# Reordering exp and the key products of a decode block's softmax part, and spreading its weight gradients over more heads

## The chip, the cores and the metric

The kernel runs on one core of one Trainium2 chip. The metric is the device time of one launch in microseconds (us), lower is better. A core has TensorE (PE, matrix products; PEld in a profile is its loading of weights), VectorE (DVE), ScalarE (ACT), GpSimd (POOL) and SyncE (SP), each with its own instruction queue that runs in order. They work in the on-chip memory SBUF; matrix products land in PSUM. Transfers between the device's memory and SBUF are issued here by SP (loads and four small stores) and by POOL (large stores); 16 DMA engines carry them.

## The reference

The block is one decode step of attention and an MLP with residuals, and what is timed is the forward pass together with the gradients of everything but one unused input. There are 2 batch entries, one query each, 32 heads, a cache of 4096 keys and values of 128 elements per head, a model width of 640 and an MLP width of 1728, all in bf16.

```python
x = A_x                                    # [2, 1, 640]
q = layernorm(x) @ wq                      # 32 heads x 128
p = softmax(q . k_cache * 128**-0.5)       # per pair (batch, head): 4096 probabilities
o = p @ v_cache
h = x + o @ wo
out = h + relu(layernorm(h) @ w1) @ w2
out, vjp = jax.vjp(f, x, k_cache, v_cache, wq, wo, w1, w2)
return out, *vjp(grad_out)
```

The gradients of the two caches are by far the largest outputs: one [4096, 128] array per pair for the keys and one for the values. For a pair they are outer products, gV = p x go and gK = gs x q * scale with gs = p * (V go - dot). The gradients of wq, wo, w1 and w2 are outer products of two vectors per batch entry, summed over the batch.

## The kernel before

Work goes by the 64 pairs of batch and head. A pair's K or V (1 MB) lies in one SBUF buffer of [128 partitions, 32 rows, 128]. Ten such buffers (`NBIG`) are shared by two classes: "ld" for loads, "g" for gradients on their way out. `take` and `give` hand them out in order; `pump` issues the next load of a fixed list as soon as a load buffer is given back in program order, and SP waits until the last reader is done.

**The first pass**, `p1_iter(i)` (L437 to 557), is a software pipeline over pairs with three in work at once: `c` is pair i (scores), `p` is pair i-1 (exponentials and products), `r` is pair i-2 (sums over values). It is a generator of eight stages, k = 0 to 7. Between two stages the caller may insert second-pass and background work, so the order of instructions on each engine is the order in which the program issues them; nothing is rescheduled (`manual_schedule`).

- K is transposed on PE in four groups of eight blocks (`transpose_group`, L373 to 383, PSUM tile `t_ps`, two buffers). Each group is copied to SBUF (`t_sb`) by ACT (L382), apart from the fourth of the first 33 iterations, which DVE copies (L380). `matvec_group` (L388) then multiplies by q, giving the scores `s`.
- Stage 1: PE sums over the rows of the scaled keys of `r` (`u_rows`, L465, one set of four products for each half of `pk`), spreads the maximum of `p` over partitions (L483), and DVE takes the minimum of it, giving the bias `nb` (L485).
- Stage 3: ACT computes `ep = exp(SCALE * s + nb)` with the sum `esum` (L502). It stands after the copy of the third key group (stage 2). At the end of stage 3 ACT copies `ep` into the column 128 of two tiles `pk` (L513).
- Stage 4: `pk_half(0)` (L452), a DVE product of half of the keys with `ep`. Stage 5: reciprocal of the total and the normalised probabilities (L533, L534). Stage 6: the maximum of `c`'s scores (L542), then `pk_half(1)`, after which the key buffer is given back.
- `m_part(0..7)` (L445) accumulates value rows against `pk` for `r`, four rows in each part, spread over all stages; stage 7 gives the value buffer back and ACT copies the result out (L553, L554).

**The second pass**, `p2_iter(j)` (L777 to 830), reads V again as a tile `Wt`. It transposes it on PE as fp32 (L398), with ACT copies (L403), multiplies it by `go` (L411), and DVE writes gK and gV by halves (L772). POOL stores them (L810, L829).

**The plan** (L1014 to 1026): iterations i = 0 to 43 run the first pass alone; from i = 44 to 65 every other iteration also carries one head of the second pass ("mixed"); the 53 other heads run by themselves ("the last part"). The first 32 pairs are batch entry 0. After i = 33 and i = 65 a background generator `middle_gen` computes attention output, layer norm, MLP, and the vector `go` of each head, which the second pass needs. Its long reductions on DVE are `ttr` (L622).

**Background work** runs by credit. `bg_step(k, rate)` adds `rate` to a queue's credit, at most 2, and lets the queue's generator run until the credit is used; each `yield` of a generator says what it used (0.5 where it says nothing). Three queues exist: `bg` (middle parts), `bg2` with the rate `RATE2` (weight gradients, `fin_gen`, L936 to 972), and `bg3` with 0.6 (`gx_gen`, the gradient of x through wq, L882 to 934). `fin_gen` starts in the last part, once the MLP of batch entry 1 is done, and goes through a fixed list:

- vectors are laid out as rows by `rows_of` (1.7 credits for four column groups: two yields of 0.5 and one of 0.7)
- `outer_rows` makes the outer products of the four weights: PE products of 2 rows (L872), ACT copies out of PSUM (L877), and a store by POOL (L879). Two products cost 1.0. The outputs come in the order out_7 (w2), out_6 (w1), out_5 (wo), out_4 (wq)
- before the rows of wo's gradient it waits for the vector `gh1` of batch entry 1, and before those of wq's for the last group of `go`
- last come the layer norm's gradient and two row stores of out_1

In the last part each head calls all three queues seven times. `gx_gen` reloads wq in six tiles `wqs` (L891) and holds each for `at[k]`, 18 steps after issue, before it transposes it (L916).

Of the kernel before, what the change touches and what calls it, by code (L numbers as in the profile page):

```python
# [7 lines left out]
FP32 = mybir.dt.float32  # L8
BF16 = mybir.dt.bfloat16
ALU = mybir.AluOpType  # L10
ACT = mybir.ActivationFunctionType
# [4 lines left out]
def kernel(  # L16
# [20 lines left out]
    nc = tc.nc  # L37
# [7 lines left out]
    NSC = Sk // 128  # L45
# [3 lines left out]
    SCALE = 0.08837890625  # L49
# [3 lines left out]
    HALF = NSC // 2  # L53
# [12 lines left out]
    small = ctx.enter_context(tc.tile_pool(name="small", bufs=3))  # L66
# [5 lines left out]
    def pst(shape, dtype, tag, name):  # L72
        return ps.tile(shape, dtype, tag=tag, bufs=PSB[tag], name=name)
# [11 lines left out]
    def balance():  # L85
        for a, b, wrong in (("ld", "g", lambda: count["ld"] > target[0]), ("g", "ld", lambda: count["ld"] < target[0])):
            while wrong() and free[a] > 0:
                homes[b].insert(0, homes[a].pop())
                for d in (free, count):
                    d[a] -= 1  # L90
                    d[b] += 1

    def take(tag, shape, name):
        assert free[tag] > 0, (tag, name)
        free[tag] -= 1
        k = homes[tag].pop(0)
        t = pools.get(k, big).tile(shape, BF16, tag=f"big{k}", bufs=1, name=name)
        home_of[id(t)] = (tag, k, t)
        return t

    def give(t):
        tag, k, _ = home_of.pop(id(t))
        free[tag] += 1
        homes[tag].append(k)
        balance()

    step = [0]
# [193 lines left out]
    pkp = tc.alloc_tile_pool(name="pkp", bufs=1)  # L301
# [83 lines left out]
    def matvec_group(dst, t_sb, g, vec):  # L385
        for j in range(GT):
            sc = g * GT + j
            nc.tensor.matmul(dst[:, sc:sc + 1], lhsT=t_sb[:, j, :], rhs=vec, start=True, stop=True)  # L388
# [48 lines left out]
    def p1_iter(i, dve_group, busy):  # L437

        c = S1[i] if i < NP1 else None
        p = S1[i - 1] if 1 <= i <= NP1 else None  # L440
        r = S1[i - 2] if i >= 2 else None

        def m_part(k):
            for sc in range(4 * k, 4 * k + 4):
                nc.tensor.matmul(r["m"][:, 0:129], lhsT=r["V"][:, sc, :],  # L445
                                 rhs=r["pk"][sc // HALF][:, sc % HALF, 0:129],
                                 start=(sc == 0), stop=(sc == NSC - 1))

        def pk_half(k):

            sl = slice(k * HALF, (k + 1) * HALF)
            nc.vector.tensor_tensor(  # L452
                out=p["pk"][k][:, :, 0:128].rearrange("p s (a two) -> p s a two", two=2),
                in0=p["K"][:, sl, :].rearrange("p s (a two) -> p s a two", two=2),
                in1=p["ep"][:, sl, None, :].to_broadcast([128, HALF, 64, 2]), op=ALU.mult)

        def u_rows(h):


            if h == 0:  # L460
                u_bank[0] = pst([128, 512], FP32, "u", "u_ps")
            for t in range(2):
                for g in range(4):
                    sc = 16 * t + 4 * g
                    nc.tensor.matmul(u_bank[0][32 * g:32 * g + 32, :], lhsT=onehot[:, 31 - h:63 - h],  # L465
                                     rhs=r["pk"][t][:, 4 * g:4 * g + 4, 0:128],
                                     start=(h == 0 and t == 0), stop=(h == H - 1 and t == 1))

        if c is not None:
            b, h = pairs[i]  # L470
            q = qc[:, h, b:b + 1]
            c["KT0"] = transpose_group(c["K"], 0, busy=busy)
            c["KT1"] = transpose_group(c["K"], 1)
        yield
        if r is not None:
            r["m"] = pst([128, 132], FP32, "m", "m_ps")
            u_rows(pairs[i - 2][1])
        if p is not None:

            bp, hp = pairs[i - 1]  # L480
            bhp = bp * H + hp
            mx = p["bank"][:, 64:192]
            nc.tensor.matmul(mx, lhsT=p["rmax"][:].to_broadcast([128, 128]), rhs=nident[:], start=True, stop=True)  # L483
            nb = small.tile([128, 1], FP32, tag="nb", name="nb")
            nc.vector.tensor_reduce(out=nb[:], in_=mx, op=ALU.min, axis=AX.X)  # L485
        if r is not None:
            m_part(0)
        yield
        if c is not None:
            c["bank"] = pst([128, 512], FP32, "sps", "s_ps")  # L490
            c["s"] = c["bank"][:, 0:NSC]
            matvec_group(c["s"], c.pop("KT0"), 0, q)
            c["KT2"] = transpose_group(c["K"], 2, busy=busy)
        if r is not None:
            m_part(1)
        yield
        if c is not None:
            matvec_group(c["s"], c.pop("KT1"), 1, q)
        if p is not None:
            ep = small.tile([128, NSC, 2], BF16, tag="ep", name="ep")  # L500
            esum = small.tile([128, 1], FP32, tag="esum", name="esum")
            nc.scalar.activation(out=ep[:], in_=p["s"][:, :, None].to_broadcast([128, NSC, 2]),  # L502
                                 func=ACT.Exp, bias=nb[:], scale=SCALE, accum_out=esum[:])
            p["ep"] = ep
        if r is not None:
            m_part(2)
        if c is not None:
            c["KT3"] = transpose_group(c["K"], 3, dve_group)
        if p is not None:
            p["pk"] = []  # L510
            for k in range(2):
                pk = pkp.tile([128, HALF, 130], BF16, tag="pK", bufs=3, name="pk")
                nc.scalar.copy(out=pk[:, :, 128:129], in_=ep[:, k * HALF:(k + 1) * HALF, 0:1])  # L513
                p["pk"].append(pk)
        yield
        if p is not None:
            pk_half(0)
        if r is not None:
            m_part(3)
        if c is not None:  # L520
            matvec_group(c["s"], c.pop("KT2"), 2, q)
        if r is not None:
            m_part(4)
        if p is not None:

            totp = p["bank"][:, 256:257]
            nc.tensor.matmul(totp, lhsT=half_f32, rhs=esum[:], start=True, stop=True)
        yield
        if r is not None:
            m_part(5)  # L530
        if p is not None:
            rtot = rt[:, bp, hp:hp + 1]
            nc.vector.reciprocal(out=rtot, in_=totp)  # L533
            nc.vector.tensor_scalar(out=P_bf[:, bhp, :], in0=ep[:, :, 0], scalar1=rtot,  # L534
                                    scalar2=None, op0=ALU.mult)
        yield
        if r is not None:
            m_part(6)
        if c is not None:
            matvec_group(c["s"], c.pop("KT3"), 3, q)  # L540
            rmax = small.tile([128, 1], BF16, tag="rmax", name="rmax")
            nc.vector.reduce_max(out=rmax[:], in_=c["s"], axis=AX.X)  # L542
            c["rmax"] = rmax
        if p is not None:
            pk_half(1)
            give(p["K"])
        yield
        if r is not None:
            br, hr = pairs[i - 2]
            m_part(7)  # L550
            give(r["V"])
            MT = mats.tile([128, 128], BF16, tag="MT", bufs=NMT, name="MT")
            nc.scalar.activation(out=MT[:], in_=r["m"][:, 0:128], func=ACT.Copy, scale=rt[:, br, hr:hr + 1])  # L553
            nc.scalar.activation(out=OU[:, br, hr, 0:1], in_=r["m"][:, 128:129], func=ACT.Copy, scale=rt[:, br, hr:hr + 1])  # L554
            MTs[(br, hr)] = MT
            del S1[i - 2]
        yield
# [324 lines left out]
    def gx_gen(fin, gx1):  # L882
# [3 lines left out]
        def load(k):  # L886
            hn = min(QP, H - k * QP)
            while free["ld"] < 1:
                yield 0.0
            tiles[k] = take("ld", [128, ND, QP * 128], "wqs")  # L890
            nc.sync.dma_start(out=tiles[k][:, :, 0:hn * 128],  # L891
                              in_=wq_r[:, :, k * QP * 128:(k * QP + hn) * 128])
            at[k] = step[0] + 18

        at = {}
        for k in range(NQ):
# [117 lines left out]
    M0_ITERS = 10  # L1014
    P2_AT = H + 2 + M0_ITERS
    RATES = (0.2, 0.6, 0.2, 0.8, 0.45)
    RATE2 = 1.0
    plan = []
    i = j = 0
    while i <= NP1 + 1 or j <= NP1:  # L1020
# [55 lines left out]
    for n, (i, j) in enumerate(plan):  # L1076
# [26 lines left out]
        if i is None:  # L1103
            spread[0] = 2
            k = 0
            while g2 is not None:
# [4 lines left out]
                bg_step(0, rate)  # L1111
                bg_step(1, RATE2)
                bg_step(2, 0.6)
            continue
        at = MIXED if j is not None else REST
        for k, _ in enumerate(p1_iter(i, i < H + 1, 2 if H + 1 < i < H + 5 else 0)):
# [14 lines left out]
            bg_step(0, rate)  # L1131
            bg_step(1, RATE2)
        if i is not None and i in (H + 1, NP1 + 1):
# [41 lines left out]
```

## Time and profile before

| What | Value |
|---|---|
| Time, median of 8 runs | 955.39 us (951.59 to 962.02) |
| Time of the profiled execution | 953.29 us |
| Its span, first to last instruction | 951.5 us |
| PE busy | 771.5 us, 81% |
| DVE busy | 654.8 us, 69% |
| ACT busy | 574.0 us, 60% |
| POOL busy | 114.1 us, 12% |
| Bytes moved | 372.37 MB, mean 391 GB/s |
| Mean granted PE clock | 0.784 |

In the page's slices each digit is the busy share of one fortieth of the span in tenths; `PEclk` is the PE clock that was granted, in tenths of full speed, and the line GB/s what the DMA engines moved. Stages in time: the first pass for batch entry 0 until about 218 us; the first pass alone beside the middle of batch entry 0 until about 310 us; the mixed part until about 490 us; the last part after that. Stores of the weight gradients (L879) run from 569.4 to 821.6 us; the two row stores of out_1 are issued at 862.5 and 877.3 us; the last gK is issued at 937.4 us.

In a list of waits each row is: engine, tile and line that waited, what released it, then total us, number of times, longest us. In the order of time each row is: start us, duration us, engine, line, operation, output and input, and in brackets the idle time of the engine before it and its releaser. In a table by stretch each engine has busy us and a count.

### The profile page before, as it was taken

Reading aid. Unit: us, or ns where it says so; the run is one execution under the profiler, and the core shown is the slowest. Engines: PE = TensorE matmul, PEld = TensorE weight load, DVE = VectorE, ACT = ScalarE, POOL = GpSimd, SP = SyncE. Lnnn points to the kernel's source line nnn. Section 1 sums busy time; section 2 is a strip of 40 time slices with the busy share of each in tenths; the row PEclk is TensorE's granted clock in tenths of the full one; section 3 lists DMA queues with packets and bytes.
Section 4 is the critical chain, followed back from the end, with each engine's and each line's share of the span. In section 5 each row is a group of like instructions: output and inputs, shape, how many; then the busy total and the mean of one; then the engine's idle time right before and its main releaser. Section 6 shows DMA issues by size and latency. Waiting matters only on the chain.

```text
span 951.5 us, 27206 instructions
## 1 busy us (share of the span) xinstructions
PE 771.5 (81%) x11643; PEld 650.9 (68%) x11643; DVE 654.8 (69%) x1235; ACT 574.0 (60%) x1250; POOL 114.1 (12%) x220
## 2 busy tenths in 40 slices
PE   5999999989888989889787888778885679856670
PEld 4888878878777878778776866565574565545560
DVE  4566877855496977868659886586499744556683
ACT  3666666657577767767534466677763568733340
POOL 1000000000000110100102211121132211121131
PEclk8999999999799999999887555575575765665565
DMA  8999999999685999999999999999999999999996
GB/s 348 409 401 404 410 404 411 408 418 386 226 306 226 361 425 422 421 403 424 399 410 399 395 423 370 362 393 421 389 404 423 421 423 421 414 424 421 417 424 287
DMA packets 62952, 372.37 MB, mean 391 GB/s; under 512 B 5776, under 2 KB 19280, under 8 KB 21232
## 3 DMA queue, kind: packets, MB, share of 16 engines
q1 hardware_dynamic: 42176, 221.50, 58.5%
q0 software_dynamic: 20656, 149.14, 37.8%
q8 instruction: 91, 1.49, 0.6%
q14 instruction: 29, 0.24, 0.1%
HBM read 221.48 MB, written 149.13 MB: 389 GB/s over the span
## 4 chain that ended last, share of the span: by engine, by line
PE 38%; DMA 25%; DVE 21%; ACT 7%; issue 7%; POOL 1%; POOLq 0%; ACTq 0%; DVEq 0%
DVE pk L452 10%; PE t_ps L398 10%; DMA out_dram<-gV 9%; DMA Vt<-in_A_v_cache_dram 6%; PE m_ps L445 6%; PE t_ps L377 6%; DMA Kt<-in_A_k_cache_dram 4%; DVE gV L772 3%; DMA wqs<-in_A_wq_dram 3%; PE o_ps L872 3%; DMA out_dram<-ot 3%; PE dp_ps L411 2%; PE s_ps L388 2%; PE u_ps L465 2%; ACT t_sb L403 2%
## 5 line engine op out<-in xcount | busy, mean ns | idle before, releaser
L382 ACT COPY t_sb<-t_ps 128x1024 bf16<-128x1024 bf16 x223 | 219.5, 1015 | 62.8 <-PE t_ps L377 61.0
L398 PE MATMUL t_ps<-ident_f,Wt 128*128 128x128 f32 x1024 | 223.9, 366 | 0.3 <-ACT t_sb L918 0.3
L445 PE MATMUL m_ps<-pk,Vt 128*128 128x129 bf16 x2048 | 197.9, 223 | 14.5 <-DMA Vt<-in_A_v_cache_dram 14.4
L403 ACT COPY t_sb<-t_ps 128x512 f32<-128x512 f32 x256 | 148.2, 588 | 91.9 <-PE t_ps L398 88.3
L398 PEld LDWEIGHTS t_ps<-ident_f,Wt 128*128 128x128 f32 x1024 | 162.6, 190 | 18.3 <-issue 8.5
L452 DVE TENSOR_TENSOR pk<-Kt,ep 128x2048 bf16<-128x2048 bf16 x128 | 156.1, 1220 | 21.0 <-ACT ep L502 20.9
L772 DVE TENSOR_TENSOR gK<-rb,gsp 128x2048 bf16<-128x2048 bf16 x128 | 152.3, 1228 | 21.1 <-DMA out_dram<-gK 19.1
L772 DVE TENSOR_TENSOR gV<-rb,pp 128x2048 bf16<-128x2048 bf16 x128 | 152.4, 1220 | 15.7 <-DMA out_dram<-gV 8.8
L377 PE MATMUL t_ps<-ident_bf,Kt 128*128 128x128 bf16 x2048 | 152.9, 225 | 3.1 <-DMA Kt<-in_A_k_cache_dram 2.9
L445 PEld LDWEIGHTS <-Vt 128*128 128x128 bf16 x2048 | 134.5, 101 | 15.9 <-DMA Vt<-in_A_v_cache_dram 15.3
L411 PEld LDWEIGHTS <-t_sb 128*128 128x128 bf16 x2048 | 93.3, 106 | 73.9 <-ACT t_sb L403 62.0
L411 PE MATMUL dp_ps<-gom,t_sb 128*128 128x2 bf16 x2048 | 95.1, 167 | 47.1 <-ACT t_sb L403 46.4
L377 PEld LDWEIGHTS <-Kt 128*128 128x128 bf16 x2048 | 126.9, 101 | 5.1 <-DMA Kt<-in_A_k_cache_dram 3.3
L829 POOL DMA_DIRECT2D out_dram<-gV x64 | 34.2, 534 | 514.1 <-DVE gV L772 427.7
L388 PE MATMUL s_ps<-qc,t_sb 128*128 128x1 bf16 x2048 | 87.9, 164 | 1.3 <-ACT t_sb L382 0.9
L388 PEld LDWEIGHTS <-t_sb 128*128 128x128 bf16 x2048 | 79.3, 97 | 3.3 <-ACT t_sb L382 2.0
L877 ACT CAST ot<-o_ps 128x512 bf16<-128x512 f32 (+4 forms) x160 | 68.5, 480 | 20.1 <-PE o_ps L872 17.6
L785 DVE SCALAR_TENSOR_TENSOR gsp<-dp_ps,negdot,P_bf 128x64 bf16<-128x64 f32 x64 | 18.0, 281 | 86.3 <-PE dp_ps L411 85.9
L799 ACT CAST rb<-dp_ps 128x256 bf16<-128x256 f32 x64 | 24.0, 375 | 79.4 <-DVE gK L772 51.7
L465 PE MATMUL u_ps<-pk,onehot 128*32 128x512 bf16 x512 | 48.5, 396 | 20.8 <-DVE pk L452 20.1
L810 POOL DMA_DIRECT2D out_dram<-gK x64 | 34.0, 532 | 238.7 <-DVE gK L772 198.0
L380 DVE COPY t_sb<-t_ps 128x1024 bf16<-128x1024 bf16 x33 | 22.8, 692 | 51.8 <-PE t_ps L377 51.8
(204 smaller groups left out, 795.7 us busy)
## 6 DMA issues: line engine op xcount, KB each, us to landing
Kt<-in_A_k_cache_dram SPq DMA_DIRECT2D x64, 1024.0 KB, 13.0
Vt<-in_A_v_cache_dram SPq DMA_DIRECT2D x64, 1024.0 KB, 13.3
Wt<-in_A_v_cache_dram SPq DMA_DIRECT2D x64, 1024.0 KB, 12.7
out_dram<-gV POOLq DMA_DIRECT2D x64, 1024.0 KB, 13.6
out_dram<-gK POOLq DMA_DIRECT2D x64, 1024.0 KB, 13.1
wo_t<-in_A_wo_dram SPq DMA_DIRECT2D x4, 1280.0 KB, 19.8
out_dram<-ot POOLq DMA_DIRECT2D x5, 1024.0 KB, 11.8
wq_t<-in_A_wq_dram SPq DMA_DIRECT2D x5, 960.0 KB, 13.9
```

What stands on the lines that cost most here:

```text
L377: nc.tensor.transpose(t_ps[:, j, :], nat[:, g * GT + j, :], ident_bf[:])
L382: nc.scalar.copy(out=t_sb[:], in_=t_ps[:])
L388: nc.tensor.matmul(dst[:, sc:sc + 1], lhsT=t_sb[:, j, :], rhs=vec, start=True, stop=True)
L398: nc.tensor.transpose(t_ps[:, j, :], natf[:, 2 * cc:2 * cc + 2, :].rearrange("p c k -> p (c k)"), ident_f[:])
L403: nc.scalar.copy(out=t_sb[:], in_=t_ps[:])
L411: nc.tensor.matmul(dst[:, sc:sc + 2], lhsT=v[:, j, :, par], rhs=vecs[:, par, :], start=(par == 0), stop=(par == 1))
L445: nc.tensor.matmul(r["m"][:, 0:129], lhsT=r["V"][:, sc, :], rhs=r["pk"][sc // HALF][:, sc % HALF, 0:129], start=(sc == 0), stop=(sc == NSC ...
L452: nc.vector.tensor_tensor(out=p["pk"][k][:, :, 0:128].rearrange("p s (a two) -> p s a two", two=2), in0=p["K"][:, sl, :].rearrange("p s (a ...
L465: nc.tensor.matmul(u_bank[0][32 * g:32 * g + 32, :], lhsT=onehot[:, 31 - h:63 - h], rhs=r["pk"][t][:, 4 * g:4 * g + 4, 0:128], start=(h == ...
L772: nc.vector.tensor_tensor(out=pairs_view(dst[:, sl, :]), in0=row.rearrange("p (a two) -> p a two", two=2)[:, None, :, :].to_broadcast([128 ...
L829: nc.gpsimd.dma_start(out=natural(out_3, b, h), in_=gV[:])
L877: nc.scalar.copy(out=ot[0:P, k, n0:n0 + nn], in_=o_ps[0:P, 0:nn])
```

## The change

Four things are moved or altered:

1. exp of `p` goes from stage 3 to the head of stage 2, ahead of the third key group's copy.
2. `pk_half(0)` goes from the head of stage 4 to the end of stage 3, in front of the yield; `pk_half(1)`, with the give-back of the key buffer, from the end of stage 6 to stage 5, in front of the reciprocal. The tile `pk` and its ACT copy are made inside `pk_half`, one at a time.
3. `RATE2` goes from 1.0 to 0.55.
4. The wait for a reloaded wq tile goes from 18 to 22 steps.

```diff
         def pk_half(k):
 
+            pk = pkp.tile([128, HALF, 130], BF16, tag="pK", bufs=3, name="pk")
+            nc.scalar.copy(out=pk[:, :, 128:129], in_=p["ep"][:, k * HALF:(k + 1) * HALF, 0:1])
+            p["pk"].append(pk)
             sl = slice(k * HALF, (k + 1) * HALF)
...
             c["s"] = c["bank"][:, 0:NSC]
-            matvec_group(c["s"], c.pop("KT0"), 0, q)
-            c["KT2"] = transpose_group(c["K"], 2, busy=busy)
-        if r is not None:
-            m_part(1)
-        yield
-        if c is not None:
-            matvec_group(c["s"], c.pop("KT1"), 1, q)
         if p is not None:
             ep = small.tile([128, NSC, 2], BF16, tag="ep", name="ep")
             esum = small.tile([128, 1], FP32, tag="esum", name="esum")
             nc.scalar.activation(out=ep[:], in_=p["s"][:, :, None].to_broadcast([128, NSC, 2]),
                                  func=ACT.Exp, bias=nb[:], scale=SCALE, accum_out=esum[:])
             p["ep"] = ep
+        if c is not None:
+            matvec_group(c["s"], c.pop("KT0"), 0, q)
+            c["KT2"] = transpose_group(c["K"], 2, busy=busy)
+        if r is not None:
+            m_part(1)
+        yield
+        if c is not None:
+            matvec_group(c["s"], c.pop("KT1"), 1, q)
         if r is not None:
             m_part(2)
         if c is not None:
             c["KT3"] = transpose_group(c["K"], 3, dve_group)
         if p is not None:
             p["pk"] = []
-            for k in range(2):
-                pk = pkp.tile([128, HALF, 130], BF16, tag="pK", bufs=3, name="pk")
-                nc.scalar.copy(out=pk[:, :, 128:129], in_=ep[:, k * HALF:(k + 1) * HALF, 0:1])
-                p["pk"].append(pk)
-        yield
-        if p is not None:
             pk_half(0)
+        yield
         if r is not None:
             m_part(3)
...
             m_part(5)
         if p is not None:
+            pk_half(1)
+            give(p["K"])
+        if p is not None:
             rtot = rt[:, bp, hp:hp + 1]
...
             c["rmax"] = rmax
-        if p is not None:
-            pk_half(1)
-            give(p["K"])
         yield
...
-            at[k] = step[0] + 18
+            at[k] = step[0] + 22
...
-    RATE2 = 1.0
+    RATE2 = 0.55
```

More of the change, by code (lines that the diff above doesn't have):

```diff
@@ L491, in p1_iter @@
             c["s"] = c["bank"][:, 0:NSC]
+        if p is not None:
+            ep = small.tile([128, NSC, 2], BF16, tag="ep", name="ep")
+            esum = small.tile([128, 1], FP32, tag="esum", name="esum")
+            nc.scalar.activation(out=ep[:], in_=p["s"][:, :, None].to_broadcast([128, NSC, 2]),
+                                 func=ACT.Exp, bias=nb[:], scale=SCALE, accum_out=esum[:])
+            p["ep"] = ep
+        if c is not None:
             matvec_group(c["s"], c.pop("KT0"), 0, q)
@@ L498, in p1_iter @@
             matvec_group(c["s"], c.pop("KT1"), 1, q)
-        if p is not None:
[L500 to L504, printed above, removed]
         if r is not None:
@@ L510, in p1_iter @@
             p["pk"] = []
-            for k in range(2):
-                pk = pkp.tile([128, HALF, 130], BF16, tag="pK", bufs=3, name="pk")
-                nc.scalar.copy(out=pk[:, :, 128:129], in_=ep[:, k * HALF:(k + 1) * HALF, 0:1])
-                p["pk"].append(pk)
+            pk_half(0)
         yield
-        if p is not None:
-            pk_half(0)
         if r is not None:
@@ L531, in p1_iter @@
         if p is not None:
+            pk_half(1)
+            give(p["K"])
+        if p is not None:
             rtot = rt[:, bp, hp:hp + 1]
@@ L543, in p1_iter @@
             c["rmax"] = rmax
-        if p is not None:
-            pk_half(1)
-            give(p["K"])
         yield
```

## The prediction

> **What bounds the kernel now.** I read the page's second part first, since its slices separate the stages.
>
> ```profile
> PE   5999999989888989889787888778885679856670
> DVE  4566877855496977868659886586499744556683
> PEclk8999999999799999999887555575575765665565
> GB/s 348 409 401 404 410 404 411 408 418 386 226 306 226 361 425 422 421 403 424 399 410 399 395 423 370 362 393 421 389 404 423 421 423 421 414 424 421 417 424 287
> ```
>
> A slice is 23.8 us. From 0 to about 230 us the DMA moves some 405 GB/s (softmax part, first 32 heads). Slices 11 to 14 (238 to 333 us) fall to 226 to 361: compute alone sets the pace. From 333 us it is mostly 421 to 425, with a second dip at 560 to 700 us. Where the DMA is full, shortening compute buys nothing; the gain must come from the dips, and from 541 us on the total is bytes over rate.
>
> Second, the busy time by stretch (columns: PE, PEld, DVE, ACT, POOL busy with counts, granted clock, DMA share, GB/s):
>
> ```profile
> 192.00:218.00 26.00, 24.71 (x466) 21.81 (x467) 14.43 (x33) 16.09 (x35) 0.00 (x0) 0.93 1.01 416
> 273.36:279.80 6.44, 6.05 (x119) 5.38 (x117) 5.91 (x18) 5.12 (x11) 0.00 (x0) 1.00 0.85 327
> 580.00:600.00 20.00, 15.74 (x132) 12.69 (x133) 12.39 (x26) 12.58 (x33) 3.55 (x8) 0.50 0.99 362
> 600.00:620.00 20.00, 15.77 (x117) 9.67 (x116) 10.27 (x14) 14.75 (x32) 3.42 (x7) 0.50 0.96 359
> 680.00:700.00 20.00, 16.96 (x158) 13.06 (x157) 13.69 (x23) 12.31 (x32) 3.95 (x8) 0.50 0.94 364
> 700.00:760.00 60.00, 40.33 (x560) 34.67 (x558) 54.89 (x84) 31.18 (x64) 15.71 (x27) 0.73 1.02 421
> ```
>
> To be seen: one softmax iteration of the first dip (6.44 us) has PE at 94% and DVE at 92%, so only a few tenths of a microsecond per iteration are loose. The DMA share cannot tell the second dip from a full queue (0.99 at 362 GB/s, 1.02 at 421), so I go by GB/s.
>
> Third, the waits of 254 to 294 us, and the order of one iteration there on ACT and DVE:
>
> ```profile
> DVE pk L452 <- ACT ep L502: 7.5, 6, 3.4
> PE u_ps L465 <- DVE pk L452: 3.2, 5, 0.9
> ...
> 270.18 1.01 ACT L382 COPY t_sb<-t_ps 128x1024 bf16<-128x1024 bf16 x1 [1.15 <-PE t_ps L377]
> 271.08 0.32 ACT L502 ACTIVATE ep<-s_ps,nb 128x64 bf16<-128x64 f32 x1
> 271.53 1.23 DVE L452 TENSOR_TENSOR pk<-Kt,ep 128x2048 bf16<-128x2048 bf16 x1 [0.47 <-ACT ep L502]
> 272.67 0.75 DVE L622 CUSTOM_DVE_ANT_0 junk<-w_t,fbc 128x576 bf16<-128x576 bf16 x1
> 273.35 0.17 DVE L533 RECIPROCAL rt<-s_ps 128x1 f32<-128x1 f32 x1
> 273.87 1.22 DVE L452 TENSOR_TENSOR pk<-Kt,ep 128x2048 bf16<-128x2048 bf16 x1
> ```
>
> The loop: third key group's copy, exp, first key product, one background reduction, three small operations, second key product, the u_rows matmuls of PE (they wait 0.39 to 0.85 us for it), the maximum, the next third group.
>
> **The change, part by part.**
>
> *Exp ahead of the third copy.* Nothing is added. The bias nb is ready at 269.59 (269.30 + 0.29); the third group's PSUM at 270.14. Exp (0.32, plus 0.20 for the accumulator read) fits ACT's 1.15 us idle time, about 269.66 to 270.18, and the copy starts about when it did. Cover gone: where nb is late the copy waits behind exp. In the first 32 heads, once background reductions run, nb ends some 0.3 us later than the copy's PSUM and the third group's matvec moves by about 0.25 us. In the mixed part (310 to 490 us) ACT is busy with the first two copies until 345.5 while nb ends at 345.35, so exp costs the copy its own 0.5 us; behind it stand the fourth copy and PE's matvec of the third group. The mixed part runs at 421 to 425 GB/s, which hides this; if it did not, 0.3 us in 11 iterations is 3 us.
>
> *First key product at once.* DVE had been free since 271.06, so of its 0.47 us wait nearly all goes. In the first 32 heads the fourth copy is on DVE (0.69 us) directly ahead of it and still is: gain nothing.
>
> *Second key product ahead of reciprocal, P and maximum.* It starts up to 0.45 us earlier there (0.16 + 0.24 + 0.19, overlapped: 71.47 against 71.02 in one iteration). The maximum now comes after it and PE's broadcast of it waits. First part, the loop from the fourth copy's start: 0.61 to the first product, 1.13 to the second, 1.14 to the reciprocal, 0.19 + 0.16 to the maximum, 0.25 to PE's broadcast, 2.27 to the next copy: 5.75 against 6.06 us, so 0.31, not 0.45. In the dip DVE's own list (1.14 + 0.68 + 0.2 + 0.15 + 0.07 + 0.10 + 1.13 + 0.74 + 0.21 + 0.79 + 0.76) is 5.97 us against 6.44: at most 0.47.
>
> *Queues.* SP's reload of a key buffer waits for this product; it moves earlier with it, and value or W loads queued behind it on SP too. No DMA is added, POOL's order is untouched. The two ones-columns copies of ACT (some 0.2 us each) split; the second needs m_part(3), which has run by then.
>
> *What reaches the end.* Up to 192 us nothing: PE waits 2.0 us there for a key load, so the DMA dates that point. From 198 to 218 us 3.5 iterations x 0.31 = 1.1 us (ceiling: PE's idle 1.3). From 254 to 293 us PE idles 0.80 + 0.38 + 0.85 + 0.39 + 0.78 + 0.76 = 3.96 us; the loop sets that idle time, but DVE stops it at 0.47 an iteration, so I take 5 x 0.46 = 2.3 us. Part one: **3.4 us, between 0 and 5.3**; zero if the layer-norm chain (236 to 254 us, PE idle 2.9) and the first W group's forced chain (293 to 302) swallow it.
>
> *Weight gradients spread.* RATE2 is the credit a background step gives. The generator's costs add to 134: 97 (out_7, out_6, out_5), then 37 (GQ rows, out_4). A head has 7 steps. Before: 97/7 = 14 heads, an idle stretch till the last GQ group (head 41), then 37/7 = 5.3 heads; the trace shows those stores from 569 to 693 us and from 792 to 822 us. After: 97/0.55/7 = 25 heads, 37/0.55/7 = 9.6: heads 17 to 53 without a gap. Nothing is added.
>
> At 560 to 700 us a head carries 6.6 units (9.95 us: 541 to 693 for 15.3 heads), and the DMA loses against 421: 26 x 20 + 59 x 20 + 62 x 20 + 17 x 20 + 57 x 20 (395, 362, 359, 404, 364 GB/s) = 4.4 MB, **10.5 us**. After, 3.85 units a head. With no units a head takes at most 6.8 us (nine heads, 693 to 754), so linearly 6.8 + 3.15 x 3.85/6.65 = 8.6 us. The DMA needs, for 36 heads of 3.15 MB, 14.9 MB of gradients and 5.2 MB of wq, 133 MB / 421 = 317 us: 8.8 a head. Compute is just under the DMA, too close to recover all: I take 0.63 of 10.5, **6.6 us**, with 10.5 above and a loss below.
>
> *Wait of 22 steps for wq.* Its PE stalls (7.4 us at 730.7, 6.5 at 755.1) shrink, but the DMA ran at 421 then: 0. It and the slower rate push the last row store from head 54 to about 60.5 of 64: 3.5 heads left. If they were gone, out_4's rest would be a tail of 10 us or more.
>
> **Two rules weighed.** Row first: 700 to 760 us moved 421 GB/s. [...] by the row 6.6 more. The row decides. Second: the clock was 0.50 at 580 to 620 us with PE 79% busy, and 0.73 at 700 to 760 with 67%. [...] the filled heads 32 to 41 run their transposes at half clock (1.09 instead of 0.64 us per four, 1.8 us a head, 18 us over ten heads). I allow half clock: the 9.95 us heads had it already.
>
> **Sum.** 3.4 + 6.6 = 10.0 us against the profiled execution's 953.3 (span 951.5 and 1.8 around it): 943.3. The median is 2.1 us above that execution, so **945.4**.
>
> **Rivals.** (1) *Spreading is hidden, only the loop gains*: 955.4 - 3.4 = 952.0. For it: the DMA share of 0.96 to 1.02 in the dip. Against: its GB/s. (2) *The loop change is hidden, spreading works*: 948.8. For it: the chain runs over PE at 218 to 236 us (PE 97% busy), and the third part takes what is left. (3) *Slower*: the filled last part becomes compute-bound. Heads 17 to 53 took 329 us, 9.1 a head; the chain matmul, ACT eviction, next matmul (PE waits 15.0 us for evictions at 560 to 700) then stands in all 36 heads, beside the W transposes at half clock. At 9.5 us a head it costs 36 x 0.4 = 14 less 3.4: 966. It decides from 9.2 us a head. For it: PE 79 to 85% busy at 0.50. Against: the linear 8.6.
>
> **How the numbers follow.** Forecast 0.55, rival 1 0.14, rival 2 0.11, rival 3 0.20. About 0.5% (4.8 us) is what this kernel's measurement can tell from no change. The forecast holds 940 to 949, almost all faster; rival 2 is faster in half of its cases; rival 1 mostly within. Faster 0.60, same 0.20, slower 0.20. The forecast's low end with all 10.5 and 5.3 is 939.6, less 2 us of spread; the high end takes rival 1 and the mild side of rival 3: 938 to 958.
>
> **What would show it.** Right: the idle time of DVE's first product on ep gone at 254 to 293 us and iterations of some 6.0 us; exp ahead of the third copy with that copy's wait unchanged; first dip 3 us shorter; gradient stores evenly from about 575 to 860 us, with 410 GB/s or more at 560 to 700; last row store well before the last gK. Wrong: ACT's third copy late behind nb, heads 32 to 53 above 9 us at less than 421 GB/s, or a slower first part.

## The result and the profile after

The changed kernel takes **945.66 us** (median of 11 runs, 941.68 to 950.13) beside 955.81 for the kernel before (32 runs); the ratio is 0.9894, 95% interval 0.987 to 0.9918. The forecast was 945.4. The total is right, but the profile shows another split of it: that the sum came out is luck. Its execution takes 945.39 us (span 943.6; before 953.29 and 951.5).

The page's slices (23.6 us each), after:

```profile
PE   5999999989899989799798866857687786766670
DVE  4666777856688968678759787766957557445683
PEclk8999999999999989999975575656755568557565
GB/s 348 409 397 407 410 405 410 407 419 410 288 308 268 407 424 421 424 391 422 421 421 334 421 422 384 383 374 412 406 424 420 422 406 421 425 409 399 423 422 262
```

The eleventh slice (236 to 260 us) has risen from 226 to 288 GB/s and its clock from 7 to 9, the fourteenth from 361 to 407. The second dip is still there (slices 25 to 27, 566 to 637 us). Busy time by stretch, after (columns as in the prediction):

```profile
192.00:218.00 26.00, 25.38 (x478) 22.21 (x479) 14.50 (x29) 17.31 (x37) 0.00 (x0) 0.94 1.02 420
254.00:293.00 39.00, 36.43 (x726) 32.64 (x724) 33.43 (x94) 30.73 (x66) 0.00 (x0) 1.00 0.72 272
...
560.00:580.00 20.00, 15.22 (x118) 11.60 (x117) 17.45 (x28) 11.19 (x27) 3.83 (x9) 0.50 1.02 414
580.00:600.00 20.00, 15.20 (x121) 11.89 (x122) 11.71 (x21) 11.73 (x29) 3.13 (x7) 0.50 1.00 370
600.00:620.00 20.00, 14.93 (x182) 12.62 (x181) 15.61 (x25) 11.50 (x31) 3.12 (x7) 0.67 1.00 372
620.00:640.00 20.00, 12.94 (x94) 8.77 (x93) 11.54 (x20) 10.98 (x23) 3.13 (x7) 0.50 0.99 386
640.00:700.00 60.00, 44.76 (x537) 36.20 (x536) 47.05 (x72) 38.39 (x92) 11.63 (x23) 0.67 1.01 413
```

The order in the loop is the intended one. ACT and DVE in one iteration of the first dip, after (start and length in us):

```profile
262.71 0.29 DVE L488 TENSOR_REDUCE nb<-s_ps 128x1 f32<-128x128 f32 x1
...
262.91 0.76 DVE L621 CUSTOM_DVE_ANT_0 junk<-w_t,fbc 128x576 bf16<-128x576 bf16 x1
...
263.03 0.31 ACT L498 ACTIVATE ep<-s_ps,nb 128x64 bf16<-128x64 f32 x1
...
263.36 1.01 ACT L382 COPY t_sb<-t_ps 128x1024 bf16<-128x1024 bf16 x1
...
264.39 1.22 DVE L455 TENSOR_TENSOR pk<-Kt,ep 128x2048 bf16<-128x2048 bf16 x1
...
266.20 1.22 DVE L455 TENSOR_TENSOR pk<-Kt,ep 128x2048 bf16<-128x2048 bf16 x1
...
267.34 0.17 DVE L535 RECIPROCAL rt<-s_ps 128x1 f32<-128x1 f32 x1
```

The exponentials run 0.33 us ahead of the third copy, and neither product waits: DVE fills the time with background reductions (the L621 lines). Where the 7.9 us of the span came from is read off the start of the maximum in each softmax iteration, and of the store of gV in each head of the second pass (trace, us; heads 0 to 10 lie in the mixed part):

| Point | Before | After | Gained so far |
|---|---|---|---|
| iteration 32 | 218.09 | 218.39 | -0.3 |
| iteration 33 | 223.78 | 222.65 | 1.1 |
| iteration 35 | 241.33 | 240.17 | 1.2 |
| **iteration 36** | 252.03 | 246.65 | **5.4** |
| iteration 42 | 293.57 | 286.22 | 7.4 |
| head 0 | 313.73 | 305.20 | 8.5 |
| head 17 | 539.07 | 531.86 | 7.2 |
| head 53 | 868.74 | 860.44 | 8.3 |
| head 63 | 934.79 | 926.87 | 7.9 |

In this pair of traces the whole gain is there by head 0. Behind that point one trace is a weak witness: the trace of the spreading alone, told below, runs the program of the kernel before up to the last part, keeps step with it up to iteration 42 (0.2 us), and is 5.8 us behind at head 10. Heads 17 to 53, over which the weight gradients now spread, take 328.6 us instead of 329.7, but not evenly: the changed kernel is 28.0 us ahead at head 32 and 7.8 at head 44. And more than half of the gain comes from a single iteration, to which the forecast gave nothing. Its stretch, first before, then after:

```profile
236.00:240.00 4.00, 3.36 (x60) 3.04 (x59) 3.13 (x21) 3.05 (x10) 0.00 (x0) 1.00 0.95 387
240.00:244.00 4.00, 1.70 (x37) 1.17 (x37) 2.90 (x6) 0.88 (x1) 0.00 (x0) 0.96 0.43 107
244.00:248.00 4.00, 4.00 (x54) 3.45 (x52) 0.82 (x1) 1.32 (x3) 0.00 (x0) 0.50 0.88 356
248.00:252.00 4.00, 4.00 (x78) 3.97 (x76) 1.40 (x7) 1.28 (x3) 0.00 (x0) 0.50 0.35 145
```

```profile
236.00:240.00 4.00, 2.57 (x46) 1.93 (x43) 3.53 (x18) 2.72 (x7) 0.00 (x0) 1.00 0.65 262
240.00:244.00 4.00, 3.94 (x94) 3.41 (x94) 1.85 (x4) 1.47 (x4) 0.00 (x0) 1.00 0.86 311
244.00:248.00 4.00, 3.68 (x88) 3.47 (x85) 2.23 (x8) 1.87 (x6) 0.00 (x0) 1.00 1.00 356
248.00:252.00 4.00, 3.12 (x61) 2.46 (x59) 0.68 (x2) 3.53 (x7) 0.00 (x0) 1.00 0.98 391
```

Before, PE is "4.00 busy" at 244 to 252 us at a granted clock of 0.50, and iteration 36 takes 10.70 us. After, the clock stays at 1.00 and it takes 6.48. What precedes it is PE's wait for the key products. PE's timeline, before and then after (the bracket is the idle time and what ended it):

```profile
241.12 0.40 PE L465 MATMUL u_ps<-pk,onehot 128*32 128x512 bf16 x4 [1.76 <-DVE pk L452]
242.70 0.40 PE L465 MATMUL u_ps<-pk,onehot 128*32 128x512 bf16 x4 [1.18 <-DVE pk L452]
```

```profile
239.96 0.40 PE L468 MATMUL u_ps<-pk,onehot 128*32 128x512 bf16 x4 [1.43 <-DVE pk L455]
```

Before, both products stand behind some twenty small layer-norm operations on DVE, and PE waits 1.76 and 1.18 us for them. After, the first product runs ahead of that chain and one wait of 1.43 us is left.

Two theories are left. **Mine after the traces**: the loop's edits give all of the gain, some 8 us, about half of it by keeping PE's clock up once (1.00 instead of 0.50 at 244 to 252 us); the spreading gives nothing, because the second dip is made by slow transfers and not by compute. **The forecast's**: 3.4 us from the loop and 6.6 from the spreading.

### The profile page after: what moved, and what is told of

Read it like the earlier page. It is cut to its first block, busy times and chain, and to the rows that moved or that the text cites. A ratio compares the mean times of both kernels' runs of the same rounds, so it can differ in the third digit from the quotient of the medians.

```text
span 943.6 us, 27268 instructions
## 1 busy us (share of the span) xinstructions
PE 765.8 (81%) x11643; PEld 647.6 (69%) x11643; DVE 655.6 (69%) x1235; ACT 573.0 (61%) x1250; POOL 112.3 (12%) x220
## 4 chain that ended last, share of the span: by engine, by line
DMA 34%; PE 31%; DVE 16%; issue 12%; ACT 4%; POOL 1%; POOLq 0%; DVEq 0%; ACTq 0%
DMA out_dram<-gV 13%; DMA Vt<-in_A_v_cache_dram 10%; PE m_ps L445 8%; PE t_ps L377 8%; DMA out_dram<-gK 7%; DVE pk L455 5%; DVE gV L771 5%; DMA out_dram<-ot 4%; PE t_ps L398 3%; PE s_ps L388 3%; DVE gK L771 2%; PE u_ps L468 2%; ACT t_sb L382 2%; PE t_ps L369 1%; DVE junk L621 1%
## 5 line engine op out<-in xcount | busy, mean ns | idle before, releaser
L398 PE MATMUL t_ps<-ident_f,Wt 128*128 128x128 f32 x1024 | 227.3, 368 | 1.4 <-ACT t_sb L917 0.7
L455 DVE TENSOR_TENSOR pk<-Kt,ep 128x2048 bf16<-128x2048 bf16 x128 | 153.0, 1223 | 18.7 <-PE m_ps L445 12.7
L552 ACT ACTIVATE MT<-m_ps,rt 128x128 bf16<-128x128 f32 x64 | 23.5, 368 | 60.3 <-PE m_ps L445 60.3
L621 DVE CUSTOM_DVE_ANT_0 junk<-wo_t,hbc 128x640 bf16<-128x640 bf16 x64 | 52.4, 818 | 0.2
```

The lines of the kernel that those rows point to most:

```text
L398: nc.tensor.transpose(t_ps[:, j, :], natf[:, 2 * cc:2 * cc + 2, :].rearrange("p c k -> p (c k)"), ident_f[:])
L455: nc.vector.tensor_tensor(out=p["pk"][k][:, :, 0:128].rearrange("p s (a two) -> p s a two", two=2), in0=p["K"][:, sl, :].rearrange("p s (a ...
L621: nc.vector.tensor_tensor_reduce(out=junk[0:kc, 0:width], in0=in0, in1=in1, scale=1.0, scalar=0.0, op0=ALU.mult, op1=ALU.add, accum_out=acc)
```

## Experiments

**The loop alone.** The changed kernel with the old rate and the old wait:

```diff
-            at[k] = step[0] + 22
+            at[k] = step[0] + 18
-    RATE2 = 0.55
+    RATE2 = 1.0
```

> The loop's changes alone: the exponentials and both key products are where the changed kernel has them, the weight gradients keep the old rate (1.0) and the old wait of 18 steps. Reading of the two traces: the loop gives nearly all of the gain, 7.5 to 9 us (4.2 of them in iteration 36, where the granted clock stays at 1.00 instead of falling to 0.50), so a time 7 to 9 us below the kernel before, within 2 us of the changed kernel. Forecast's split: 3.4 us, at most 5.3. Seen in its profile: if the first, the start of iteration 45's maximum lies 8 us earlier than before and the last part takes as long as before.

Measured: 947.3 us beside 958.16 before, ratio 0.9882 (0.9852 to 0.9911): 10.9 us by the medians, as much as the whole change, and above the 5.3 that the forecast held possible. Its trace, of its fastest run, has gained 8.8 us by head 0, of which 5.2 by iteration 36.

**The spreading alone.** The kernel before with RATE2 = 0.55 and 22 steps.

> The spreading alone: the loop is the old one, the weight gradients get the rate 0.55 and the wait of 22 steps. Forecast's split: 6.6 us faster. Reading of the two traces: heads 17 to 53 take 329 us either way, so no gain, within 2 us of the kernel before, with the slow stretch (under 400 GB/s) only moved later, to 580 to 640 us, where the 96-partition stores of out_7 are.

Measured: 958.34 us beside 958.16, ratio 1.000 (0.998 to 1.0019). The spreading is worth nothing, within 2 us. Its busy time by stretch:

```profile
580.00:600.00 20.00, 10.47 (x85) 8.80 (x86) 16.77 (x31) 9.09 (x22) 4.12 (x9) 0.50 1.01 390
600.00:620.00 20.00, 15.93 (x154) 12.63 (x152) 10.38 (x16) 12.86 (x31) 2.87 (x7) 0.62 1.00 379
620.00:640.00 20.00, 10.60 (x121) 8.36 (x122) 15.72 (x24) 6.80 (x22) 2.90 (x7) 0.64 1.01 391
```

PE is busy for only half of two of these slices, so PE is no bound there; the DMA share is 1.00 to 1.01 all the same, at 379 to 391 GB/s. The engines are full and move too little. And what the thinner heads win is lost again where the units now stand, first before, then with the spreading:

```profile
820.00:880.00 60.00, 40.10 (x456) 34.25 (x454) 37.56 (x51) 24.23 (x50) 11.88 (x24) 0.61 1.01 419
820.00:880.00 60.00, 41.74 (x354) 29.15 (x355) 26.55 (x32) 35.40 (x69) 9.74 (x20) 0.52 0.98 389
```

Worked out from the bytes moved, as in the prediction, the kernel before loses 10.5 us against 421 GB/s at 560 to 700 us and 0.1 at 760 to 880. The spreading alone loses 7.2 and 5.4 there, the changed kernel 7.9 and 2.5. The loss moved; it didn't go away.

**Which edit of the loop.** One run leaves the second product at its old place, one moves only the second product:

```diff
# without the second product's move (loop alone as base)
-            pk_half(1)            # ahead of the reciprocal
-            give(p["K"])
...
+            pk_half(1)            # after the maximum
+            give(p["K"])
```

> The loop's changes without the second key product's move: exponentials ahead of the third copy and the first product at once, the second product and the release of the key buffer back behind the maximum; rate 1.0, wait 18. If the first product ahead of the layer-norm chain is what kept the clock up, the 4.2 us of iteration 36 are here, and with the 1 to 2 us of the first product's wait the time is 5 to 7 us below the kernel before. If the second product's move is what matters, 0 to 2 us below. Forecast's sizes: the first product's wait 0.47 us in 5 to 6 iterations of the dip, about 2 us.

> The kernel before with one edit: the second key product and the release of the key buffer ahead of the reciprocal, the scaling and the maximum; exponentials and first product stay at their old places. The loop alone gave 10.9 us, the loop without this move 6.6, so by difference the move is worth 4 us, if the two parts add. By the forecast's sizes it is worth 0.31 us in 3.5 iterations and less than 0.47 in 6 more, so 1 to 3 us. If it only works where the first product is early already, 0.

Measured: 951.56 us (0.9924, 0.9895 to 0.9953) without it, 949.99 us beside 957.41 (0.9929, 0.9908 to 0.9949) with it alone: 6.6 and 7.4 us. Each gives more than half, and the 1 to 3 us by the forecast's sizes was too small. Their sum, 14.0, is above the 10.9 of both together; the intervals are too wide to tell the two apart, but the traces show what the edits share: in each of them PE's wait at 240 us is shorter in sum (1.87 us, and 1.76 + 0.74) than the 2.94 before, and the spell of half clock shrinks to some 3 us. By the trace, iterations 35 and 36 together take 18.23 us without the second product's move and 17.73 with it alone, 20.69 before and 16.38 with both: 2.5 and 3.0 us apart, 4.3 together.

**Is it the clock?** The products come earlier and the clock stays up; two runs separate these. The first fills PE's wait of the kernel before with matmuls that nobody reads (the kernel has two such fillers in each of iterations 34 to 36 already, L369), and reorders nothing. In a first attempt they stood one iteration too early:

```diff
-            c["KT1"] = transpose_group(c["K"], 1)
+            c["KT1"] = transpose_group(c["K"], 1, busy=6 if i == H + 3 else 0)
```

> The kernel before with six extra matmuls of 512 columns, whose result nobody reads, ahead of the second key group's transposes in the one iteration that stands behind the layer-norm chain (about 240 us); nothing is reordered. If the clock is what iteration 36 lost, PE stays busy over the gap, the granted clock at 244 to 252 us is 1.00 instead of 0.50, iteration 36 takes about 6.5 us instead of 10.7 and the time is about 4 us (at least 2.5) below the kernel before. If the order of the work was what mattered there (products waiting behind the layer-norm chain), the fillers change nothing or cost their own 1.3 us.

Measured: 956.0 us, 0.9976 (0.9953 to 1.0). PE's waits at 240 us were still 1.76 and 1.18 us and the clock fell to 0.50; it tells nothing on the theory. With `busy=8 if i == H + 4` they stand in the wait:

> The kernel before with eight extra matmuls of 512 columns (0.21 us each), whose result nobody reads, now directly ahead of PE's 1.76 us wait at 239.35 us: in the first run of this kind they ran one iteration too early, PE's wait stayed 1.76 us and the clock fell all the same. Nothing is reordered, and the products still come as late as before. If the idle time drops the clock, 244 to 252 us run at a granted clock of 1.00, iteration 36 takes 6.5 to 8 us instead of 10.7 and the time is 3 to 4 us below the kernel before. If the late products themselves cost the time, nothing is gained (0 to +1 us).

Measured: 953.97 us beside 957.41, ratio 0.9986 (0.996 to 1.0011). By the time alone this is no proof: the interval holds nothing as well as 3.4 us. Its trace, by stretch:

```profile
240.00:244.00 4.00, 2.79 (x49) 1.85 (x47) 2.95 (x6) 1.02 (x2) 0.00 (x0) 1.00 0.32 92
244.00:248.00 4.00, 3.95 (x102) 3.76 (x101) 1.45 (x3) 2.60 (x6) 0.00 (x0) 1.00 0.92 369
248.00:252.00 4.00, 3.52 (x67) 2.92 (x64) 2.29 (x8) 2.50 (x5) 0.00 (x0) 1.00 0.46 162
```

The clock stays at 1.00, iteration 36 takes 7.91 us instead of 10.70, and head 0 starts 3.4 us earlier. So useless work that keeps PE busy takes 2.8 us out of this iteration, with the products as late as before: that much is the clock. The other 1.5 us that the changed kernel gains in iterations 35 and 36 (17.89 against 16.40) are the order itself.

The second run goes the other way: in a kernel with the loop's edits (and other stores, told below) DVE computes the second product three times in the iteration ahead of the wait.

```diff
-            pk_half(1)
+            pk_half(1, 3 if i == H + 3 else 1)
```

> The fastest kernel so far (the loop's changes with the 128-partition stores of out_7, 939.97 us) with the second key product computed three times instead of once in the one iteration ahead of PE's wait at about 240 us; the two extra products (1.13 us each of DVE) write the same values. PE's wait there grows from some 1.4 us to some 3.7. If idle time costs its own length, the time rises by 2.3 us. If it also drops the clock as in the kernel before (0.50 at 244 to 252 us), iteration 36 takes some 12 us instead of 6.5, and the time rises by 5 to 6 us.

Measured: 944.62 us (942.18 to 946.56) against 939.97 (938.39 to 942.66) without the extra products, ratios to the kernel before of 0.9872 and 0.9833 (intervals 0.984 to 0.9905 and 0.9799 to 0.9867, which overlap). That is 4.7 us by the medians and 3.7 by the ratios, between the 2.3 of the idle time alone and the 5 to 6 with the clock, so it takes the trace to decide. Its timeline of PE:

```profile
242.61 0.40 PE L469 MATMUL u_ps<-pk,onehot 128*32 128x512 bf16 x4 [3.94 <-DVE pk L456]
```

and its stretches:

```profile
244.00:248.00 4.00, 4.00 (x55) 3.45 (x53) 1.23 (x1) 1.08 (x2) 0.00 (x0) 0.50 0.89 365
248.00:252.00 4.00, 4.00 (x78) 3.97 (x77) 2.12 (x7) 1.28 (x3) 0.00 (x0) 0.50 0.55 170
```

Iteration 35 is 2.5 us longer, the idle time's own price, and iteration 36, in which nothing was added, 2.8 us longer (9.27 against 6.49) at half clock. Taking the idle time out and putting it in gave the same 2.8 us. The 12 us expected for iteration 36 were 2.7 too many: even the kernel before takes only 10.70, and the order's part of that is spared here.

**Is the second dip the stores?** In the packets of the trace, those of out_7's three stores, which cover 96 partitions, took 420 ns each before and 452 after, while the same 7680 bytes took 292 in out_5's stores from 128 partitions. (By trace, the mean for 96 partitions lies between 373 and 469 ns in the eight traces with these stores.) So out_7 was cut into 13 groups of 128 rows and one of 64 (14 matmul units in place of 18; the expectation's "18 stores" should read 18 units in three stores):

```diff
-        yield from outer_rows(FIN["ar"], Dff, FIN["gr"], D, out_7, Dff // 96)
+        yield from outer_rows(FIN["ar"], NFF * 128, FIN["gr"], D, out_7[0:NFF * 128, :], NFF)
+        yield from outer_rows(FIN["ar"], F_rem, FIN["gr"], D, out_7[NFF * 128:Dff, :], 1, NFF * 128)
```

> The changed kernel with the gradient out_7 (1728 rows) stored from 128 partitions (1664 rows) and 64 rows in a store of their own, instead of 18 stores from 96 partitions; 14 units of matmul and eviction instead of 18. If the slow packets of the 96-partition stores (452 ns for 7680 B against 293) make the dip of 578 to 640 us, the rate there rises to 410 GB/s or more and the time is 4 to 7 us below the changed kernel. If compute makes the dip, only the four units fewer count: 1 to 2 us. If the DMA has no dip to give back, 0.

> The same stores of out_7 in the kernel with the loop's changes alone (rate 1.0, wait 18), where the units come thickest. If the 96-partition packets are what the dip is, 4 to 7 us below the loop alone (947.3), and spreading on top of it still gives nothing (within 2 us of the changed kernel with these stores). If compute bounds the thick heads, the dip stays under 400 GB/s here, while the spread form of it rises, and the two differ by 4 us or more.

Measured: 941.02 us with the spreading (0.9849, 0.9814 to 0.9883) and 939.97 without (0.9833, 0.9799 to 0.9867), 4.6 and 7.3 us below the same kernels with the old stores by the medians, 0.45 and 0.49% by the ratios. The second is the fastest kernel of this study. The two don't differ from each other, so with good stores too the spreading gives nothing. The one without it, with its thick heads (those that carry many units), by stretch:

```profile
560.00:580.00 20.00, 16.33 (x133) 11.55 (x132) 13.93 (x25) 13.73 (x34) 4.73 (x10) 0.50 1.01 415
580.00:600.00 20.00, 15.87 (x118) 10.19 (x116) 11.04 (x18) 14.82 (x34) 3.15 (x7) 0.50 1.01 414
600.00:620.00 20.00, 16.27 (x195) 13.84 (x194) 16.53 (x26) 15.45 (x41) 3.70 (x8) 0.74 1.01 400
...
640.00:660.00 20.00, 15.96 (x111) 9.76 (x109) 12.80 (x21) 13.95 (x35) 3.78 (x9) 0.50 1.00 389
660.00:680.00 20.00, 17.05 (x173) 12.88 (x170) 6.33 (x12) 13.75 (x33) 2.38 (x5) 0.50 0.98 371
680.00:700.00 20.00, 15.77 (x235) 13.45 (x233) 19.89 (x30) 12.53 (x23) 4.89 (x9) 0.86 1.01 395
```

At 580 to 600 us PE is as busy and its clock as low as in the dip of the kernel before (15.7 us and 0.50 at 362 GB/s), yet 414 GB/s flow. From 640 to 700 us, with out_7 long stored, the rate is low all the same.

Units and stores changed together, so two more runs keep the 14 units and cut only each 128-partition store in two:

```diff
-            nc.gpsimd.dma_start(out=out_v[:, c0:c0 + gn, :], in_=ot[0:P, 0:gn, :])
+            for a, z in (((0, 96), (96, 128)) if cc == NFF else ((0, P),)):
+                nc.gpsimd.dma_start(out=out_v[a:z, c0:c0 + gn, :], in_=ot[a:z, 0:gn, :])
```

> The same fastest kernel, with each 128-partition store of out_7 issued as two: partitions 0 to 95 and partitions 96 to 127. Same matmuls, evictions, bytes and packets, only the shape of the stores differs. If the shape of a 96-partition store is what makes its packets slow, the dip under 390 GB/s is back at 560 to 620 us and the time rises by 3 to 6 us. If the gain came from the four units fewer[...], the time stays within 1.5 us.

> As the run with 96 and 32 partitions, but split at partition 64. If what slows a store is that it covers the partitions unevenly, [...] the 7680-byte packets take 450 ns or more and the time rises by 5 us or more. If only counts that aren't a power of two are slow, the packets stay near 310 ns and the time within 1.5 us.

Measured: 949.55 us (ratio 0.9909, 0.9874 to 0.9945) cut at 96 and 947.87 us (0.9907, 0.9873 to 0.9942) cut at 64, 9.6 and 7.9 us above the uncut stores by the medians, 0.76 and 0.74% by the ratios. The low rate is back; cut at 96, by stretch:

```profile
560.00:580.00 20.00, 14.22 (x111) 9.45 (x110) 7.48 (x12) 12.05 (x31) 4.36 (x10) 0.50 1.01 375
580.00:600.00 20.00, 7.90 (x71) 5.92 (x72) 11.52 (x24) 6.97 (x19) 2.21 (x6) 0.59 0.88 317
600.00:620.00 20.00, 16.73 (x137) 12.08 (x136) 11.56 (x15) 14.96 (x35) 4.22 (x9) 0.50 0.92 358
```

The packets of 560 to 620 us, worked out from the trace (7680-byte packets of out_7; mean time of one, and the rate of all traffic):

```
stores of out_7        packets  mean ns   GB/s
96 (loop alone)        288      442       366
128                    256      318       409
96 + 32                256      451       351
64 + 64                256      524       364
```

At equal matmuls, evictions and bytes, the shape of three stores costs some 7 us. A store cut in two is also one store more, and no run adds stores without changing their shape; but the whole stores from 96 partitions are slow too (442 ns). The fewer partitions the larger store covered, the longer the packets took: 318 ns with 128, 442 and 451 with 96, 524 with 64. A second store for the remaining 32 partitions did not make up for it (451 beside 442). What makes these packets slow, no run shows.

The stores are not the whole dip of the kernel before. Its packets of out_7 run from 575 to 605 us, and 4.3 of the 10.5 us lost lie there (with the uncut stores from 128 partitions, 0.3). Of the rest, 680 to 700 us (364 GB/s) has none of them, and over 4 us from 616 and from 688 us the DMA share is only 0.83 and 0.74, at 273 and 208 GB/s: there the DMA engines stood idle for a part of the time, which the 0.96 and 0.94 of the 20 us stretches hide. The waits of 560 to 700 us, before and then after:

```profile
POOL out_dram L810 <- DVE gK L772: 44.4, 13, 7.1
...
DVE gV L772 <- DMA out_dram<-gV: 1.2, 1, 1.2
```

```profile
POOL out_dram L809 <- DVE gK L771: 56.4, 15, 9.5
...
DVE gK L771 <- DMA out_dram<-gV: 13.7, 6, 3.6
ACT ot L876 <- DMA out_dram<-ot: 9.2, 2, 7.1
```

Summed over the engines, all waits for a transfer are 2.0 us before, 35.8 with the spreading alone and 50.2 after. So the thinner heads do wait for the DMA, as the forecast had it, and the thick ones hardly do. This alone doesn't name the bound of the thick ones, since nothing waits for a transfer at 540 to 560 us either, at 425 GB/s. In the two runs with cut stores the engines wait 41.0 and 16.6 us for transfers at 560 to 620 us, against 2.3 with the stores uncut. What makes the part of the dip that isn't the stores was not tried.

## Why the prediction was right in sum and wrong in its parts

That the sum came within 0.3 us of the measured time is luck. The loop was put 7.5 us too low (3.4 against 10.9 by the medians) and the spreading 6.6 us too high (6.6 against 0), and the two errors cancel.

**First 32 heads, 1.1 us: right in size, not in place.** Iterations 30 to 32 take 17.63 us instead of 18.31, 0.22 us less each where 0.31 were forecast, and the iteration ahead of them, which waits for a key load, ends 1.0 us later than before. What is left at 224 us comes from iteration 33, which the forecast didn't count: the first in which ACT makes the fourth copy. DVE's wait for the exponentials falls from 1.94 to 0.47 us there, and the iteration takes 4.26 us instead of 5.69.

**First dip, 2.3 us: right.** Iterations 37 to 42 took 41.54 us before and 39.57 after: 2.0. The last five of them take 6.2 us in the mean (255.24 to 286.22), where some 6.0 were forecast. The wait of the products for the exponentials fell from 7.5 us in six places to 3.5 in two, and the maximum now gates PE in a few iterations, as the sum had allowed for. Two rows of the waits of 248 to 286 us, after:

```profile
DVE pk L455 <- ACT ep L498: 3.5, 2, 2.1
...
PEld L486 <- DVE rmax L544: 1.6, 4, 0.4
```

**The layer-norm stretch, nothing: this step failed.** The prediction named the stretch (236 to 254 us, PE idle 2.9) only as something that may swallow the gain. It gave 4.2 us, 2.8 of them by the clock. All pieces were in the trace of before: PE's two waits, the products' place behind the chain, and the 0.50 right after. The clock was weighed for the last part alone (0.50 at 580 to 620 us, 0.73 at 700 to 760), and not for this stretch, where compute is the bound. With these 4.2 us the loop's sum is 1.1 + 2.3 + 4.2 = 7.6, against 8.5 by head 0 in the trace and 10.9 by the medians; the rest is open.

**Spreading, 6.6 us: this step failed.** It is 0, within 2 us. The stores spread as forecast (571 to 861 us), and the rate at 560 to 700 us came to some 397 GB/s in the mean instead of 410 or more. Two terms were wrong. The first is in the sentence "The DMA share cannot tell the second dip from a full queue, so I go by GB/s": it charged all of the 4.4 MB missing against 421 GB/s to compute. Packets of 420 ns in place of 292 were part of it, and fewer matmuls in a head didn't shorten those (452 ns in the changed kernel). The second is that the forecast gave the heads that get filled no price (its third rival did), since 8.6 us of compute lie under the DMA's 8.8. Of the 10.5 us the changed kernel won back 2.6 at 560 to 700 us and lost 2.4 more than before at 760 to 880. With out_7 from 128 partitions the same is seen more clearly: the spread kernel loses 1.6 us at 560 to 700 and 8.3 at 760 to 880, the one without it 7.0 and 0.3. Why the filled heads run below 421 GB/s was not tried.

**The row of 421 GB/s.** The forecast took the rate of 700 to 760 us as what the dip could reach. That was near: once the stores covered 128 partitions, 400 to 417 GB/s went through each 20 us slice of 560 to 640 us without any spreading. But the stores' shape brought it, and not the spreading, with which the changed kernel moved 370 to 414 there.

**The wait of 22 steps, 0: nothing against it.** Together with the rate it changed nothing; by itself it was not tried. The last row store went out at 891.87 us, at head 57, some three heads earlier than forecast, and no tail came of it.

**Rivals.** The first one's premise (the spreading gains nothing) holds, with a loop gain of 8.5 us or more in place of 3.4. The second and third fall: the loop isn't hidden, and heads 17 to 53 stayed at 9.1 us each.

## What to carry to other kernels

When the DMA share is near 1 at a low rate (here 1.00 at 370 GB/s), look at the time of one packet by store and at the share over a few us before you blame compute: three stores of 2.2 MB in all that left partitions out cost more here (4.6 us and more) than the spreading of the work won (0). Work that is moved out of full stretches can have a price in the stretches that it fills (here a loss of 5.4 us instead of 0.1 at 760 to 880 us). Where compute is the bound, price PE's idle time together with the clock of the matmuls behind it (here 2.8 us), and look for a long chain of small operations ahead of what PE waits for.

## What the runs showed that was not expected

**The clock fell behind a short wait.** PE's waits at 240 us, and what the granted clock was in the 4 us stretches from 240 to 252:

| Kernel | PE's waits, us | Clock at 240, 244, 248 |
|---|---|---|
| before | 1.76 + 1.18 | 0.96, 0.50, 0.50 |
| before, wait filled | 1.18 | 1.00, 1.00, 1.00 |
| only the second product moved | 1.76 + 0.74 | 0.70, 0.87, 1.00 |
| without the second product's move | 1.87 | 0.68, 0.89, 1.00 |
| changed | 1.43 | 1.00, 1.00, 1.00 |
| changed, 128-partition stores | 1.42 | 0.75, 0.82, 1.00 |
| product computed three times | 3.94 | 0.97, 0.50, 0.50 |

Behind waits of 1.87 us or more in sum it fell each time, and behind one of 1.42 us once: the changed loop kept its clock in five traces of six with this wait and lost it for some 3 us in one (iteration 36 then took 7.83 us instead of 6.48). The spells at half clock in these rows lasted 3.4 us or 10.2 us by the clock records of the traces, nothing between. So the 2.8 us are on an edge, and a given execution of the changed kernel may miss part of them. What decides it from one execution to the next was not tried.

**One small tensor shapes a stage.** out_7 is 2.2 MB of 372, and with the loop alone its 288 packets of 96 partitions took 442 ns each, where out_5's from 128 partitions took 292 in the kernel before: by estimate 150 ns too long, 2.7 us spread over 16 engines. The measured price, 4.6 us and more, is about twice that. It is not because these stores slow the loads: with the loop alone the loads' packets of 8192 bytes took 366 ns at 560 to 620 us against 314 at 640 to 700, but with out_7 from 128 partitions 333 and 379. What makes up the rest is open.
